# Fused attention and two expert layers on one core: the order of the parts inside a pair of attention heads

## The chip, the cores and the metric

The kernel runs on one core of a Trainium2 chip. The metric is device time in microseconds (us), the median of several executions. The core has five engines that run side by side, each through its own queue in order: TensorE (PE, matmuls; PEld is its weight load), VectorE (DVE), ScalarE (ACT), GpSimd (POOL) and SyncE (SP, which here only issues DMAs). They wait for one another by semaphores.

## What is computed

The reference is an attention over 2 batches of 8 heads, followed by a gated layer and a layer of eight experts. The part that matters here is the attention, which keeps 576 of 1152 queries (each the mean of two neighbours):

```python
q_pool = q.reshape(B, H, S // 2, 2, D).mean(axis=3)      # B, H, S, D = 2, 8, 1152, 64
scores = matmul(q_pool, k.transpose(0, 1, 3, 2)) / sqrt(D)
attn = exp(scores - max(scores, axis=-1))
attn = attn / (sum(attn, axis=-1) + 1e-9)
x = matmul(attn, v)                                       # then reshaped to 1152 x 512
```

After it come `rms`-normalisation, a gated layer (512 to 1536 to 512) and the experts. All inputs and outputs are float32.

## The kernel before

The attention works on eight pairs of heads (`for p in range(NPB)`, line 420), four pairs for each batch. Keys are split into 9 blocks of 128 (`KC`), the 576 queries of a head into 2 groups of 288 (`NG`), so a pair has 18 steps (`NST`). Step i does `st_exp` (lines 197 to 204): for each of the two heads two matmuls into one of three PSUM banks `st`, and an exponential on ACT from that bank into the tile `et`. The score's row maximum is subtracted through an extra column of `Ql`: `s1` (line 182) computes a block of 128 queries against all keys into one single buffer of three banks, and DVE's reduction at line 193 takes the maximum. The next `s1` can only start when that reduction has ended.

Around each `st_exp` other parts are laid. Each step has two places, an even one straight after `st_exp` and an odd one at its end, so there are 36 slots; the tables `S_...` (lines 400 to 416) give the slot of each part:

- `kq_trans` (line 148) transposes keys and queries of the next pair on PE through a single PSUM bank, tag `T`, and ACT evacuates it. `ql_trans` and `ql_trans2` do the same with `Ql`.
- `split` (line 127) splits keys and queries of the pair after the next into a rounded part and a rest: five POOL instructions for each head (lines 108 to 123).
- `esum` (line 207) adds the `et` tiles up; `S_EP` says which of the nine blocks POOL adds (1) and which DVE adds (0). `emerge` (line 219) adds POOL's sum to DVE's, `sums` and `sums2` bring the sums into place.
- `avmm` (line 223) multiplies values by `et` into one bank `av`. It runs in bursts, at the steps with `c % 3 == S_AV`, and takes all `et` tiles up to two steps before (`S_LAG`). In the trace each of its matmuls is two instructions, so a step's two heads are four.
- For the first batch, `x1` (line 273), `xr` (line 293), `x2` and `x2b` turn the result into the next layer's input during pairs 4, 5 and 6 (counted from 0). `x1` and `x2b` use the bank `T` too. `xr` holds a chain of six short instructions: one on DVE, a power on POOL, four on DVE.
- During pair 7, the last one, the next layer's first weights are decoded: `w_dec` (line 380) does for one matrix an absolute value on ACT (step 0), four DVE instructions (steps 1 to 3), and a rounding copy on ACT with a subtraction on POOL (step 4). The work tile `wm` has one buffer there.

After the eight pairs the gated layer starts with matmuls `gv` (line 528); `sums` and `sums2` of the last pair come into its first slots. Its order and the experts' are not part of the change.

Of the kernel before, what the change touches and what calls it, by code (L numbers as in the profile page):

```python
# [9 lines left out]
F32 = mybir.dt.float32  # L10
# [11 lines left out]
def fused_kernel(ctx, tc, q, k, v, w_gate, w_val, w_out, rms_g,  # L22
                 r_gate, r_noise, noise, e_w1, e_w2, out, dbg=None):
    nc = tc.nc
    P = 128
    B, H, S, D = q.shape
    NP = H // 2
# [5 lines left out]
    NG = 288  # L33
# [28 lines left out]
    NPB = B * NP  # L62
# [4 lines left out]
    ab = ax.enter_context(tc.tile_pool(name="ab", bufs=1))  # L67
# [127 lines left out]
    xT, rs, es, ET, AV, accp, smS = {}, {}, {}, {}, {}, {}, {}  # L195

    def st_exp(p, g, c):
        et = ET[p, g, c] = ab.tile([P, 2, NG], F32, name="et", tag="et", bufs=7)
        cs, n0 = slice(c * P, (c + 1) * P), g * NG
        for h in range(2):  # L200
            t = ps[0].tile([P, 512], F32, name="st", tag="st", bufs=3)
            pe.matmul(t[:, 0:NG], KT[p, h][:, cs], QhT[p, h][:, n0:n0 + NG], start=True, stop=False)  # L202
            pe.matmul(t[:, 0:NG], KT2[h][p % NKT[h]][:, cs], QlT[p, h][:, n0:n0 + NG], start=False, stop=True)  # L203
            act.activation(et[:, h, :], t[:, 0:NG], AF.Exp, scale=SCALE)  # L204

    def esum(p, g, c):
# [58 lines left out]
    XS, SS, YY = {}, {}, {}  # L265
# [27 lines left out]
    def xr(b):  # L293
        ss, y = SS[b], YY[b]
        dve.tensor_scalar(y[:, 0], ss, 1.0 / (H * D), 1e-6, op0=ALU.mult, op1=ALU.add)
        pool.tensor_tensor(y[:, 1], y[:, 0], mhalf, op=ALU.pow)
        dve.tensor_tensor(y[:, 2], y[:, 1], y[:, 1], op=ALU.mult)
        dve.tensor_tensor(y[:, 2], y[:, 2], y[:, 0], op=ALU.mult)
        dve.tensor_scalar(y[:, 2], y[:, 2], -0.5, 1.5, op0=ALU.mult, op1=ALU.add)
        dve.tensor_tensor(y[:, 2], y[:, 2], y[:, 1], op=ALU.mult)  # L300
# [96 lines left out]
            act.copy(hi, mf)  # L397
            pool.tensor_tensor(lo, mf, hi.bitcast(F32), op=ALU.subtract)  # L398

    S_S1A = (0, 3, 13, 18, 22)  # L400
    S_S1B = (7, 9, 26, 27, 32)
    S_KA = (1, 3, 6, 9)
    S_KB = (4, 21, 22, 20)
    S_QA = (14, 32)
    S_QB = (24, 33)
    S_SPA = 11
    S_SPB = 24
    S_EM = (2, 21)
    S_SUM = (11, 17)
    S_LD = (4, 34, 34)  # L410
    S_AV = 1
    S_X = (31, 2, 8, 24, 26, 34)
    S_X2 = (4, 8, 20, 24)
    S_EP = (1, 1, 0, 0, 0, 1, 0, 0, 1)
    S_EV = (1, 1, 1, 0, 1, 0, 1, 0)
    S_LAG = 2
    S_W = (0, 0, 13, 26)
    EPL = [[c for c in range(KC) if S_EP[c] == z] for z in range(2)]
    av_q, n_av = [], 0
    for p in range(NPB):  # L420
        F = [[] for _ in range(2 * NST)]

        def at(i, f, *a):
            F[i].append((f, a))

        if p + 1 < NPB:
            at(S_LD[0], load_v, p + 1)
            for i in range(2, QC):
                at(S_S1A[i], s1, p + 1, 0, i - 2)
                at(S_S1B[i], s1, p + 1, 1, i - 2)  # L430
            for i in range(4):
                at(S_KA[i], kq_trans, p + 1, 0, i)
                at(S_KB[i], kq_trans, p + 1, 1, i)
            at(max(S_KA), kt2_copy, p + 1, 0)
            at(max(S_KB), kt2_copy, p + 1, 1)
            at(S_QA[1], ql_trans, p + 1, 0)
            at(S_QB[1], ql_trans, p + 1, 1)
        at(S_S1A[0], s1, p, 0, 3)
        at(S_S1B[0], s1, p, 1, 3)
        at(S_S1A[1], s1, p, 1, 4)  # L440
        at(S_QA[0], ql_trans2, p)
# [12 lines left out]
        if p:
            at(S_EM[0], emerge, p - 1, 1)
            at(S_SUM[0], sums, p - 1)
            at(S_SUM[1], sums2, p - 1)
        at(S_EM[1], emerge, p, 0)
        if p == NP:
            at(S_X[0], x1, 0, 0)  # L460
        if p == NP + 1:
            for i in range(1, QC):
                at(S_X[i], x1, 0, i)
            at(S_X[5], xr, 0)
        if p == NP + 2:
            for t, s_ in enumerate(S_X2):
                at(s_, x2, 0, t)
                at(s_ + 4, x2b, 0, t)
        if p == NPB - 1:
            fr_s.close()  # L470
            wps.append(ctx.enter_context(tc.tile_pool(name="wp", bufs=1, side="right", reuse_waits="tile")))
            for i in range(2):
                at(S_W[0], w_load, 0, i)
                for k_ in range(5):
                    at(S_W[1 + i] + 2 * k_, w_dec, 0, i, k_)
                at(S_W[1 + i] + 6, w_load, 1, i)
            for k_ in range(4):
                at(min(S_W[3] + 2 * k_, 35), w_dec, 1, 0, k_)
        for i in range(NST):
            g, c = divmod(i, KC)  # L480
            st_exp(p, g, c)
            av_q.append((p, g, c))
            for f, a in F[2 * i]:
                f(*a)
            if len(av_q) > 1:
                esum(*av_q[-2])
            if c % 3 == S_AV:
                while n_av < len(av_q) - S_LAG:
                    avmm(*av_q[n_av])
                    n_av += 1  # L490
            for f, a in F[2 * i + 1]:
                f(*a)
# [731 lines left out]
    Y_XR = 9  # L1224
# [243 lines left out]
```

## Time and profile before

| | us |
|---|---|
| median of 3 runs (830.9 to 833.09) | 831.72 |
| the profiled execution | 833.25 |
| span of its instructions | 831.1 |
| PE busy in the span | 788.2 (95%) |
| DVE busy | 578.8 (70%) |
| ACT busy | 421.3 (51%) |
| POOL busy | 304.1 (37%) |

The span is counted from the first to the last instruction, and a trace's times are from its start. Times below come from this one execution. A matmul's row lasts longer than its share of the engine, since the next one starts before it ends; how fast PE goes is read from start to start. "Granted clock" is the share of TensorE's full 2.4 GHz that the core was given in a stretch; it has two levels here, 1.0 and 0.5. A row of a stretch gives from and to, the length, then busy us (and instructions) of PE, PEld, DVE, ACT and POOL, the granted clock, the DMA engines' share and GB/s.

### The profile page before, as it was taken

The page shows a single profiled execution, that of the slowest core. Times are in us where ns is not written, and L with a number is a line of the kernel's source. Part 1 is how long each engine was busy: PE and PEld are TensorE (multiplying, and loading weights), DVE is VectorE, ACT ScalarE, POOL GpSimd, SP SyncE. Part 2 cuts the span into 40 slices and gives each one's busy share as a digit, 9 for nine tenths or more (in the row PEclk, how much of TensorE's full clock was granted, in tenths as well). Part 3 has the DMA queues.
Part 4 walks back from the last instruction along what each step waited for, and adds up shares of the span by engine and source line. Part 5 has one row for each costly group of instructions (what it writes and reads, how often), then busy time and mean ns, then how long its engine had stood idle before and what let it go on. Part 6 is the DMA issues. An engine that isn't in the chain of part 4 may idle for free.

```text
span 831.1 us, 14029 instructions
## 1 busy us (share of the span) xinstructions
PE 788.2 (95%) x5282; PEld 678.8 (82%) x5282; DVE 578.8 (70%) x838; ACT 421.3 (51%) x823; POOL 304.1 (37%) x251
## 2 busy tenths in 40 slices
PE   5999999999898889999999999999999999999992
PEld 4877777777676679999999999889989899998992
DVE  6668667677679676657588737598577869687750
ACT  4655655656566555352233343455465656566530
POOL 8747647648324451222122200102142413424431
PEclk9999999999999899999999999999999999999996
DMA  7345222131131211333123014558989779797311
GB/s 210 85 135 155 51 96 83 47 97 29 41 120 51 101 52 52 100 103 102 52 101 106 1 52 141 182 199 298 368 281 307 268 254 347 229 363 257 106 52 43
DMA packets 72939, 118.83 MB, mean 143 GB/s; under 512 B 7582, under 2 KB 37278, under 8 KB 72864
## 3 DMA queue, kind: packets, MB, share of 16 engines
q1 hardware_dynamic: 67504, 101.55, 37.9%
q0 software_dynamic: 5360, 16.31, 5.6%
q8 instruction: 43, 0.70, 0.3%
q14 instruction: 32, 0.26, 0.1%
HBM read 103.66 MB, written 10.77 MB: 138 GB/s over the span
## 4 chain that ended last, share of the span: by engine, by line
PE 72%; DVE 10%; issue 5%; ACT 4%; POOL 4%; DMA 3%; another core or an unknown queue 1%; POOLq 0%; DVEq 0%; ACTq 0%
PE gv L528 14%; PE py L1100 13%; PE ph L1073 11%; PE po L549 7%; PE av L229 7%; PE st L202 4%; PE s L188 3%; PE st L203 3%; PE tt L135 2%; PE ph L1088 2%; DMA xg<-XD,gidx 2%; DVE Ql L193 1%; PE xt L973 1%; DVE es L217 1%; ACT et L204 1%
## 5 line engine op out<-in xcount | busy, mean ns | idle before, releaser
L528 PE MATMUL gv<-XN,ws 128*128 128x256 f32 (+1 forms) x1152 | 167.4, 298 | 4.1 <-ACT sl L536 3.8
L528 PEld LDWEIGHTS gv<-XN,ws 128*128 128x128 f32 x1152 | 159.1, 190 | 10.1 <-ACT sl L536 4.0
L1006 DVE TENSOR_TENSOR wz<-raw,wz 128x1024 fp32r<-128x1024 f32 x112 | 134.1, 1222 | 14.2 <-ACT wz L106 10.5
L193 DVE TENSOR_REDUCE Ql<-s 128x1 fp32r<-128x1152 f32 x72 | 97.3, 1355 | 58.3 <-PE s L188 44.5
L1100 PE MATMUL py<-wz,hTT 128*128 128x512 f32 x552 | 134.1, 394 | 0.0
L204 ACT ACTIVATE et<-st 128x288 f32<-128x288 f32 x288 | 103.3, 413 | 53.9 <-PE st L203 49.4
L106 ACT CAST wz<-raw 128x1024 fp32r<-128x1024 f32 x112 | 113.5, 1046 | 8.0 <-PE py L1100 8.0
L1100 PEld LDWEIGHTS py<-wz,hTT 128*128 128x128 f32 x552 | 100.7, 188 | 20.2 <-DVE hTT L978 0.6
L398 POOL TENSOR_TENSOR ws<-wm,ws 128x1024 fp32r<-128x1024 f32 x18 | 43.3, 2405 | 150.2 <-ACT ws L397 96.3
L202 PE MATMUL st<-QH,KT 128*128 128x288 f32 x288 | 91.7, 333 | 5.5 <-ACT et L204 4.0
L1073 PEld LDWEIGHTS ph<-xgT,wz 128*128 128x128 f32 x768 | 92.5, 189 | 0.6
L1073 PE MATMUL ph<-xgT,wz 128*128 128x256 f32 x768 | 92.7, 281 | 0.0
L549 PE MATMUL po<-ws,hT 128*128 128x512 f32 x324 | 83.0, 395 | 0.1
L203 PE MATMUL st<-QlT,KT 128*128 128x288 f32 x288 | 82.3, 300 | 0.0
L229 PE MATMUL av<-et,v 128*64 128x288 f32 x576 | 81.9, 420 | 0.0
L202 PEld LDWEIGHTS st<-QH,KT 128*128 128x128 f32 x288 | 55.4, 193 | 20.8 <-ACT et L204 11.5
L217 POOL TENSOR_TENSOR accp<-accp,et 128x576 f32<-128x576 f32 x32 | 48.4, 1513 | 57.3 <-ACT et L204 36.7
L1134 POOL DMA_INDIRECT out_dram<-yo,sidx x23 | 33.1, 1441 | 95.4 <-DVE yo L1133 46.5
L549 PEld LDWEIGHTS po<-ws,hT 128*128 128x128 f32 x324 | 58.4, 188 | 10.7 <-ACT hT L538 0.5
L538 ACT CAST hT<-sl 128x256 fp32r<-128x256 f32 (+1 forms) x48 | 20.8, 433 | 89.4 <-DVE sl L537 89.4
L229 PEld LDWEIGHTS av<-et,v 128*64 128x64 f32 x576 | 37.5, 138 | 26.0 <-issue 5.9
L203 PEld LDWEIGHTS st<-QlT,KT 128*128 128x128 f32 x288 | 55.9, 194 | 0.0
(250 smaller groups left out, 1137.3 us busy)
## 6 DMA issues: line engine op xcount, KB each, us to landing
raw<-in_moe_w_dram SPq DMA_DIRECT2D x112, 512.0 KB
wraw<-in_moe_w_gate_dram SPq DMA_DIRECT2D x6, 1024.0 KB
wraw<-in_moe_w_val_dram SPq DMA_DIRECT2D x6, 1024.0 KB
wraw<-in_moe_w_out_dram SPq DMA_DIRECT2D x6, 1024.0 KB
kraw<-in_k_dram SPq DMA_DIRECT2D x16, 288.0 KB
v<-in_v_dram SPq DMA_DIRECT2D x8, 576.0 KB
KT<-KT SPq DMA_DIRECT2D x16, 288.0 KB
Qraw<-in_q_dram SPq DMA_DIRECT2D x16, 256.0 KB
```

The lines of the kernel that those rows point to most:

```text
L106: act.copy(o, i)
L193: dve.tensor_reduce(Ql[p % 3][h][:, c, D:D + 1], t[:, :, 0:384], axis=AX.XY, op=ALU.max, negate=True)
L202: pe.matmul(t[:, 0:NG], KT[p, h][:, cs], QhT[p, h][:, n0:n0 + NG], start=True, stop=False)
L203: pe.matmul(t[:, 0:NG], KT2[h][p % NKT[h]][:, cs], QlT[p, h][:, n0:n0 + NG], start=False, stop=True)
L204: act.activation(et[:, h, :], t[:, 0:NG], AF.Exp, scale=SCALE)
L217: eng.tensor_tensor(acc, acc, e, op=ALU.add)
L229: pe.matmul(av[h * D:(h + 1) * D, 0:NG], V[p][:, h, c, :], ET[p, g, c][:, h, :], start=(c == 0), stop=(c == KC - 1))
L528: pe.matmul(t[:, 0:n], w[a][:, d, j * P:(j + 1) * P], XN[hf][b_][:, d, cs], start=(k_ == 0), stop=(k_ == 11))
L549: pe.matmul(pt, HT[f, hf][a][:, j, c0:c0 + P], w[b_][:, j, :], start=(k_ == 0), stop=(k_ == 5))
L1006: eng.tensor_tensor(lo, RAW[u % 2][i], hi.bitcast(F32), op=ALU.subtract)
L1073: pe.matmul(o, w[a][:, d, j * P:j * P + P], XT[u][c][:, d], start=z + d == 0, stop=z == 2 and d == 3)
L1100: pe.matmul(PL[u, "y", k], x[c][:, f0 + d, k * P:k * P + P], w[a][:, d], start=i == 4 and z + d == 0, stop=i == 7 and z == 2 and d == 1)
```

## The change

Nothing is computed otherwise, and the same instructions run on PE and ACT. Six things change:

1. The tables of slots have new numbers for nearly all parts.
2. `S_AV` is now a list of steps, (1, 5, 10, 13): four bursts of values' matmuls in a pair instead of six. They cover 6, 4, 5 and 3 steps; in the first pair there are three. `et` gets nine buffers instead of seven.
3. `S_EP` gives block 0 to DVE, so POOL adds two instructions fewer in a pair, and DVE two more.
4. `xr` is cut in two: its first two instructions stay in pair 5, the four last ones (`xr2`) come in pair 6 (`S_XR = 41` is slot 5 of pair 6).
5. The last pair has its own slots (`S_LAST`), with five bursts.
6. The weights' steps in the last pair have slots of their own (`S_W`); ACT's rounding copies are further from DVE's last step before them.

The core of the diff:

```diff
-        et = ET[p, g, c] = ab.tile([P, 2, NG], F32, name="et", tag="et", bufs=7)
+        et = ET[p, g, c] = ab.tile([P, 2, NG], F32, name="et", tag="et", bufs=9)
...
         pool.tensor_tensor(y[:, 1], y[:, 0], mhalf, op=ALU.pow)
+
+    def xr2(b):
+        y = YY[b]
         dve.tensor_tensor(y[:, 2], y[:, 1], y[:, 1], op=ALU.mult)
...
-    S_SPA = 11
-    S_SPB = 24
+    S_SPA = 24
+    S_SPB = 20
...
-    S_AV = 1
-    S_X = (31, 2, 8, 24, 26, 34)
+    S_AV = (1, 5, 10, 13)
+    S_X = (26, 10, 26, 27, 30, 33)
+    S_XR = 41
...
-    S_EP = (1, 1, 0, 0, 0, 1, 0, 0, 1)
+    S_EP = (0, 1, 0, 0, 0, 1, 0, 0, 1)
...
-    S_W = (0, 0, 13, 26)
+    S_W = ((1, 3, 4, 5, 8), (12, 18, 19, 20, 27), (30, 31, 32, 34))
+
+    S_LAST = dict(s1a=(0, 9), s1b=(12,), qa=(15,), em=(16, 28), sum=(20, 35), av=(1, 5, 7, 13, 16))
...
-            if c % 3 == S_AV:
+            if i in sl["av"]:
```

What stands in a row on the engines shows it best. **PE, the first burst of a pair in the middle** (`st` are the scores, `tt` a transpose, `av` the values' matmuls). Before:

```order
L202 MATMUL st<-QH_101,KT 128x288
L203 MATMUL st<-QlT,KT_00_97 128x288
L202 MATMUL st<-QH_101,KT 128x288
L203 MATMUL st<-QlT,KT_01_99 128x288
L229 MATMUL av<-et,v 64x288 x6
L135 MATMUL tt<-identr,khl 128x128 x4
```

The same place in the changed program, with the burst behind a transpose of queries:

```order
L202 MATMUL st<-QH_102,KT 128x288
L203 MATMUL st<-QlT,KT_10_98 128x288
L202 MATMUL st<-QH_102,KT 128x288
L203 MATMUL st<-QlT,KT_11_100 128x288
L135 MATMUL tt<-identr,qh_1297 128x128 x4
L229 MATMUL av<-et,v 64x288 x12
```

The burst at the start of a pair has twelve matmuls instead of six; the transpose of keys that came behind it has gone elsewhere.

**DVE, from the end of pair 5 into pair 6** (`yy` is the chain of `xr`, `Ql` the reduction after an `s1`). Before:

```order
L217 TENSOR_TENSOR es<-es,et 128x2x288
L295 TENSOR_SCALAR yy_2100<-ss_2099 128x5
L297 TENSOR_TENSOR yy_2100<-yy_2100 128x5
L298 TENSOR_TENSOR yy_2100<-yy_2100 128x5
L299 TENSOR_SCALAR yy_2100<-yy_2100 128x5
L300 TENSOR_TENSOR yy_2100<-yy_2100 128x5
L217 TENSOR_TENSOR es<-es,et 128x2x288
L193 TENSOR_REDUCE Ql_91<-s_2587 128x1
```

In the changed program the row begins with the chain's first instruction, and the reduction stands inside the chain:

```order
L295 TENSOR_SCALAR yy_2071<-ss_2070 128x5
L217 TENSOR_TENSOR es<-es,et 128x2x288
L193 TENSOR_REDUCE Ql_91<-s_2585 128x1
L300 TENSOR_TENSOR yy_2071<-yy_2071 128x5
L301 TENSOR_TENSOR yy_2071<-yy_2071 128x5
L302 TENSOR_SCALAR yy_2071<-yy_2071 128x5
L303 TENSOR_TENSOR yy_2071<-yy_2071 128x5
```

The four instructions that need POOL's power have moved behind pair 6's first reduction.

**ACT, the second weight matrix in the last pair** (`wm` is the absolute value, `ws` the rounding copy, `et` the exponentials). Before:

```order
L387 ACTIVATE wm<-wraw 128x1024
L204 ACTIVATE et<-st 128x288 x2
L181 CAST QlT<-tt 128x2x192
L204 ACTIVATE et<-st 128x288 x6
L234 COPY xT<-av 128x288
L397 CAST ws<-wm 128x1024
```

In the changed program the same two instructions, `wm` first and `ws` last, stand further apart:

```order
L390 ACTIVATE wm<-wraw 128x1024
L204 ACTIVATE et<-st 128x288 x2
L181 CAST QlT<-tt 128x2x192
L204 ACTIVATE et<-st 128x288 x6
L248 COPY smS<-sm 128x320
L204 ACTIVATE et<-st 128x288 x6
L234 COPY xT<-av 128x288
L400 CAST ws<-wm 128x1024
```

Between the absolute value and the rounding copy there are now fourteen exponentials, where there were eight.

## Rows read from the trace of the kernel before

**Rows 1.** The page: busy time of each engine.

```profile
PE 788.2 (95%) x5282; PEld 678.8 (82%) x5282; DVE 578.8 (70%) x838; ACT 421.3 (51%) x823; POOL 304.1 (37%) x251
```

**Rows 2.** Stretches: pairs 2 and 4 to 7; busy us by engine, then clock.

```profile
80.96:112.38 31.42, 31.15 (x224) 23.59 (x223) 22.55 (x24) 18.87 (x53) 19.12 (x16) 1.00 0.27 77
...
143.81:176.72 32.91, 31.64 (x229) 23.88 (x228) 24.45 (x27) 19.43 (x55) 20.38 (x17) 1.00 0.25 73
176.72:210.45 33.73, 33.20 (x241) 25.15 (x239) 24.59 (x28) 21.52 (x61) 25.26 (x20) 1.00 0.14 36
210.45:248.75 38.30, 34.96 (x241) 26.69 (x239) 27.11 (x34) 23.57 (x61) 9.62 (x7) 0.96 0.29 87
248.75:282.64 33.89, 28.79 (x175) 19.41 (x175) 29.53 (x28) 19.90 (x47) 14.64 (x8) 0.90 0.19 63
```

**Rows 3.** Timeline, PE, around bursts: start, us, instruction.

```profile
83.07 0.29 PE L203 MATMUL st<-QlT,KT 128*128 128x288 f32 x1
83.29 1.68 PE L229 MATMUL av<-et,v 128*64 128x288 f32 x12
84.90 0.53 PE L135 MATMUL tt<-identr,khl 128*128 128x128 f32 x4
...
96.47 0.40 PE L202 MATMUL st<-QH,KT 128*128 128x288 f32 x1
96.71 0.30 PE L203 MATMUL st<-QlT,KT 128*128 128x288 f32 x1
96.84 0.29 PE L202 MATMUL st<-QH,KT 128*128 128x288 f32 x1
...
121.14 1.19 PE L229 MATMUL av<-et,v 128*64 128x288 f32 x8
```

**Rows 4.** Timeline, PE, a wait between two steps of pair 2.

```profile
103.40 0.29 PE L203 MATMUL st<-QlT,KT 128*128 128x288 f32 x1
103.81 0.40 PE L202 MATMUL st<-QH,KT 128*128 128x288 f32 x1
```

**Rows 5.** Timeline, ACT, six exponentials in a row; behind the time, the idle before them.

```profile
138.93 2.11 ACT L204 ACTIVATE et<-st 128x288 f32<-128x288 f32 x6 [2.70 <-PE st L203]
```

**Rows 6.** Timeline, PE, pair 4, behind the first `x1`.

```profile
173.85 0.45 PE L135 MATMUL tt<-identr,Ql 128*128 128x128 f32 x3 [1.00 <-DVE xs L286]
```

**Rows 7.** Timeline, DVE and PE at the start of pair 6.

```profile
212.37 1.38 DVE L297 TENSOR_TENSOR yy<-yy 128x5 f32<-128x5 f32 x1 [1.31 <-POOL yy L296]
...
217.50 0.62 PE L190 MATMUL s<-KT,QH 128*128 128x384 f32 x1 [2.59 <-DVE Ql L193]
```

**Rows 8.** A stretch just after it (columns as in group 2).

```profile
218.00:220.00 2.00, 2.00 (x8) 2.00 (x7) 0.35 (x2) 0.00 (x0) 0.00 (x0) 0.50 0.00 0
```

**Rows 9.** Timeline, all engines, the last pair.

```profile
256.20 0.79 PE L188 MATMUL s<-KT,QH 128*128 128x384 f32 x3 [1.21 <-DVE Ql L193]
...
259.69 2.38 POOL L398 TENSOR_TENSOR ws<-wm,ws 128x1024 fp32r<-128x1024 f32 x1 [6.09 <-ACT ws L397]
259.72 2.97 DVE L215 TENSOR_TENSOR es<-et 128x576 f32<-128x576 f32 x1
...
271.30 1.05 ACT L397 CAST ws<-wm 128x1024 fp32r<-128x1024 f32 x1 [2.93 <-DVE wm L394]
...
272.71 0.61 PE L202 MATMUL st<-QH,KT 128*128 128x288 f32 x1 [3.80 <-ACT et L204]
```

**Rows 10.** Stretch from the last pair's start to its `sums` (columns as in group 2).

```profile
248.75:287.09 38.34, 33.24 (x209) 22.90 (x207) 31.20 (x30) 22.44 (x51) 16.30 (x9) 0.91 0.25 83
```

**Rows 11.** Groups by line: additions of `et` tiles; busy, mean ns, idle before.

```profile
L217 POOL TENSOR_TENSOR accp<-accp,et 128x576 f32<-128x576 f32 x32 | 48.4, 1513 | 57.3 <-ACT et L204 36.7 <-DVE es L217 14.0 <-DVE rs L261 4.8
...
L217 DVE TENSOR_TENSOR es<-es,et 128x576 f32<-128x576 f32 x48 | 46.7, 974 | 2.3
```

**Rows 12.** Timeline, POOL: first and last of one `split`'s five instructions.

```profile
123.11 1.02 POOL L108 TENSOR_SCALAR khl<-kraw 128x576 fp32r<-128x576 f32 x1 [5.90 <-PE tt L135]
...
127.13 1.11 POOL L123 TENSOR_TENSOR Ql<-qs,qh 128x256 fp32r<-128x256 f32 x1
```

More of the change, by code (lines that the diff above doesn't have):

```diff
@@ L398, in w_dec @@
             pool.tensor_tensor(lo, mf, hi.bitcast(F32), op=ALU.subtract)
[L400 to L405, printed above, removed]
[L406 to L415 removed]
+    S_S1A = (1, 6, 16, 13, 20)
+    S_S1B = (10, 5, 21, 26, 28)
+    S_KA = (0, 5, 2, 7)
+    S_KB = (8, 18, 12, 20)
+    S_QA = (14, 29)
+    S_QB = (15, 33)
+    S_SPA = 24
+    S_SPB = 20
+    S_EM = (12, 33)
+    S_SUM = (17, 22)
+    S_LD = (4, 34, 34)
+    S_AV = (1, 5, 10, 13)
+    S_X = (26, 10, 26, 27, 30, 33)
+    S_XR = 41
+    S_X2 = (6, 22, 27, 31)
+    S_EP = (0, 1, 0, 0, 0, 1, 0, 0, 1)
     S_LAG = 2
[L417 removed]
+    S_W = ((1, 3, 4, 5, 8), (12, 18, 19, 20, 27), (30, 31, 32, 34))
+    S_LAST = dict(s1a=(0, 9), s1b=(12,), qa=(15,), em=(16, 28), sum=(20, 35), av=(1, 5, 7, 13, 16))
     EPL = [[c for c in range(KC) if S_EP[c] == z] for z in range(2)]
@@ L437, in fused_kernel @@
             at(S_QB[1], ql_trans, p + 1, 1)
[L438 to L441, printed above, removed]
+        sl = S_LAST if p == NPB - 1 else dict(s1a=S_S1A, s1b=S_S1B, qa=S_QA, em=S_EM, sum=S_SUM, av=S_AV)
+        at(sl["s1a"][0], s1, p, 0, 3)
+        at(sl["s1b"][0], s1, p, 1, 3)
+        at(sl["s1a"][1], s1, p, 1, 4)
+        at(sl["qa"][0], ql_trans2, p)
         if p + 2 < NPB:
@@ L454, in fused_kernel @@
         if p:
[L455 to L458, printed above, removed]
+            at(sl["em"][0], emerge, p - 1, 1)
+            at(sl["sum"][0], sums, p - 1)
+            at(sl["sum"][1], sums2, p - 1)
+        at(sl["em"][1], emerge, p, 0)
         if p == NP:
@@ L464, in fused_kernel @@
             at(S_X[5], xr, 0)
+        if p == NP + 1 + S_XR // 36:
+            at(S_XR % 36, xr2, 0)
         if p == NP + 2:
@@ L471, in fused_kernel @@
             wps.append(ctx.enter_context(tc.tile_pool(name="wp", bufs=1, side="right", reuse_waits="tile")))
[L472 to L478, printed above, removed]
+            at(0, w_load, 0, 0)
+            at(0, w_load, 0, 1)
+            for i, a in enumerate(((0, 0), (0, 1), (1, 0))):
+                for k_, s_ in enumerate(S_W[i]):
+                    at(s_, w_dec, *a, k_)
+                if i < 2:
+                    at(S_W[i][3], w_load, 1, i)
         for i in range(NST):
@@ L1251, in fused_kernel @@
     at(Y_XR, xr, 1)
+    at(Y_XR, xr2, 1)
     for i, a in enumerate([(1, 4), (0, 4), (1, 0), (1, 1), (1, 2), (1, 3)]):
```

## The prediction

> **What bounds the kernel now.** I read the page first: PE is busy for 95% of the span [rows 1], so only what PE does or waits for between its matmuls can shorten the attention. Then the stretches pair by pair [rows 2]. A pair in the middle takes 31.42 us; pair 4 takes 32.91, pair 5 33.73, pair 6 38.30, and the last one 33.89 although it prepares no further pair and has a fourth fewer matmul instructions (175 against 224). The clock column says the same: 1.00 in pairs 2, 4 and 5, 0.96 in pair 6, 0.90 in pair 7. So the steady pairs are bounded by PE's own order of work, and pairs 6 and 7 by long waits with a slow clock behind them. Third, PE's timeline tells what a burst of values' matmuls costs beside its work and which waits are left [rows 3, 4, 6]; last, the timelines of pairs 6 and 7 say whom PE waits for [rows 7, 9].
>
> **Bursts.** A burst of twelve instructions takes 84.90 - 83.29 = 1.61 us from its start to the next part's [rows 3]. The piece with eight of them lasts 1.19 against 1.68, so four (one step's two heads) take 0.49 and twelve 1.47: 0.14 is the burst's own. Entering costs 0.09 (0.22 from the last score matmul at 83.07, where 0.13 is the usual distance, 96.71 to 96.84), leaving 0.11 (0.24 from 96.47 to 96.71). A burst costs 0.34 us beside its work. Pairs 0 to 6 have 5 + 6 x 6 = 41 bursts before and 3 + 6 x 4 = 27 now: 14 x 0.34 = 4.8. Pair 0 also hands three more steps on, which end up in pair 7, where I count them again: 3 x 0.49 = 1.5. **Gain 6.2.** That nothing is merged is excluded: the changed order shows bursts of twelve, eight, ten and six.
>
> **Longer stretches without a burst.** In a burst ACT and DVE catch up; outside one, a step of scores alone takes PE 4 x 0.13 = 0.53 us, but its two exponentials take ACT 2 x 2.11 / 6 = 0.70 [rows 5]. There are three `st` banks, so PE waits: in pair 2 0.28 us at 103.40 (0.41 between two starts less 0.13) [rows 4], one of three such waits in the pair, 0.19 to 0.28 each and 0.74 in all. I laid the changed slots out step by step with these durations. Between the bursts of steps 13 and 1 stand six steps, and I find waits of 0.3 and 0.5; `s1` comes twice within two or three steps (steps 3 and 5, 6 and 8) and waits some 0.1 each for the reduction to free its only buffer, and a transpose 0.2 for bank `T`: 1.2, so 0.45 more than today. Bounds: all waits vanish (0.74 gained), or each of 14 steps without a burst costs its 0.17 in full (14 x 0.17 = 2.4, 1.7 more than today). I take 0.45, by the waits of 0.19 to 0.28 that are already there. Six pairs: **loss 2.7** (gain 4.4 to loss 10).
>
> **Additions moved from POOL to DVE.** Two per pair. DVE has 31.42 - 22.55 = 8.9 us idle in a pair; the work of the two is 2 x 0.97 = 1.9 [rows 2, 11]. They are followed by reductions, for which `s1` waits; that is in the step-by-step count above. POOL loses 2 x 1.51. Cost nothing in pairs 0 to 6, hidden by DVE's idle time; without that cover 1.9 a pair. The same addition is 0.5 us shorter on DVE than on POOL. The Trainium skill (Perfetto Trace Analysis, section Optimizing Scalar/DVE Operations) speaks against such a move: the two engines share an SBUF port, so shifting work between them might not help. By that rule DVE would not lose the 1.0 us of blocked time that is taken off in the last pair below; that pair would gain 3.8 instead of 4.8, and the median would come to 820.5.
>
> **`x1` in pairs 4 and 5.** In pair 4 `x1` stands one slot ahead of `ql_trans`, both in bank `T`, and PE waits 1.00 us for DVE to empty it [rows 6]. Now a burst (1.61), a step of scores and an `s1` lie between, more than DVE's reduction and multiplication: **gain 1.0** (0 to 1.2). In pair 5 two `x1` have only one step or one burst behind them, and DVE stands in its reductions: between 0 and two waits like that of pair 4, I take 0.6: **loss 0.6** (0 to 2).
>
> **`xr` cut in two, pair 6.** DVE waited 1.31 us for POOL's power inside the chain, which ran long itself (1.38 for a 128 x 5 tile), and the reduction behind it came so late that PE idled 2.59 us for `Ql` [rows 7]. Behind that the clock was 0.50, its lower level of 1.2 GHz [rows 8]; the pair's column loses 0.04 of 38.30 us, 1.5 [rows 2]. What is queued behind the chain now is the reduction of slot 6, not that of slot 1: before it PE has the twelve-matmul burst (3.1 us by the prices above) and two steps. POOL has done its splits and products some 2 us before by my count. **Gain 2.6 + 1.5 = 4.1** (0 if POOL is later). `x2b` at slots 31 and 35 again shares bank `T` with `ql_trans` at 33 and adds evacuations to the burst-free stretch: **loss 0.6** (0 to 2).
>
> **The last pair.** Here two waits stand: 1.21 us for a reduction behind weights' work on DVE, and 3.80 for an exponential that stood behind ACT's rounding copy, which itself waited 2.93 for DVE [rows 9]. The clock loses (1 - 0.91) x 38.34 = 3.4 up to the `sums` of this pair [rows 10]. Without all three PE would be there after 38.3 - 5.0 - 3.4 = 29.9; one burst less (-0.3), three steps more (+1.5), and within the burst of step 13, which crosses from the first group of queries to the second, a wait for ACT to empty `av` (I take 0.6, by the 0.70 that two exponentials take there [rows 5]) make 31.7. But `sums` also needs DVE to be through with the pair's additions and three matrices' steps. DVE is busy for 31.20 of the 38.34 [rows 10]; it gets 1.9 more and loses about 1 that it spent blocked behind POOL: an addition that began with POOL's 2.38 took 2.97 [rows 9] where 0.97 is the mean [rows 11]. With some 1.4 until the first reduction DVE ends at 31.2 + 1.9 - 1.0 + 1.4 = 33.5. So DVE is what comes late next, and PE reaches `sums` after 33.5, not 31.7: **gain 38.3 - 33.5 = 4.8**. Bounds: 31.7 gives 6.6; with DVE idle for 3.6 (half of today's 7.1) and no less blocked it is 36.7 and gives 1.6.
>
> **Sum.** 6.2 - 2.7 + 1.0 - 0.6 + 4.1 - 0.6 + 4.8 = 12.2 us off the profiled execution's own 833.25 (its span of 831.1 and 2.15 around it, which stays): 821.05. That execution lies 1.53 above the median of the runs, 831.72, so the median should come to **819.5**. The gated layer and the experts keep their order; the slots that follow `sums` hang on it and shift with it.
>
> **Rivals.**
> - *The waits stay in the last pair.* ACT's rounding copy of the second matrix again waits for DVE, or the absolute value of the third waits for POOL's subtraction (one `wm` buffer). For: DVE is the fuller engine there, and POOL and DVE block each other [rows 9]. Against: the copy stands six slots further from DVE's step. The last pair then gains 0.8 instead of 4.8: 823.5. The Trainium skill (SBUF — State Buffer, section Who interferes with whom) states that a DVE instruction with two SBUF inputs and a reading GpSimd one exclude each other for their whole length; it would make this case likelier, and the 2.97 us row agrees.
> - *POOL's power is late in pair 6.* The wait of 2.6 and its slow clock stay: 819.5 + 4.1 = 823.6. For: POOL is fullest in pair 5 (25.26 us) [rows 2]; against: three additions there become two in each group.
> - *Better than counted.* No added waits in the steady pairs, pairs 5 and 6, and the last pair bounded by PE: 819.5 - 2.7 - 1.2 - 1.8 = 813.8.
> - *Slower.* The two `split` now stand at steps 10 and 12 instead of 5 and 12, one behind the other on POOL, with an addition behind. One takes 5.13 us (123.11 to 128.24) [rows 12], two 10.3, with the addition (1.51) 11.8; from step 10, at some 17.5 us of 31, they end at 29.3. The next pair transposes them in its slots 0 and 2, from 31 on. If POOL is slowed by DVE until both take over 15 us, PE waits at the start of each of six pairs; it decides from 2.5 us a pair on (12.2 gained and 2.5 for a slower verdict, over six). At 3 us: 819.5 + 18 = 837.5. Against: POOL's share of a pair is 19.12 of 31.42 and falls.
>
> **How the numbers follow.** Forecast with its own spread (816 to 822.5) 0.52; waits stay in the last pair 0.18; power late 0.08; better 0.13; slower 0.05; gains and losses within 0.3% of no change 0.04. A measurement of this kernel can tell about 0.3%, 2.5 us, from no change. Faster 0.91, same 0.04, slower 0.05. The range for 8 in 10 takes in the better case down to 812 and both cases of waits that stay, together with a steady loss near the middle of its bounds, up to 827.
>
> **What would show it.** Pairs 1 to 3 at about 31.1 us each, with bursts of 24, 16, 20 and 12 instructions; no wait above 1 us for `Ql` at the start of pair 6 and a clock of 1.00 there; pair 4 near 31.9; in the last pair no wait above 2 us and a clock of 0.97 or more, and `sums` behind DVE's last merge. I am wrong if steady pairs take over 31.4 (the longer stretches cost more than the bursts), if PE waits for `khl` at a pair's start, or if the clock falls again in pairs 6 or 7.

## The result, and the profile after

| | before | changed |
|---|---|---|
| median of 4 runs each, us | 832.04 (830.9 to 833.09) | 821.94 (817.62 to 823.64) |
| the profiled execution, us | 833.25 | 823.6 |
| its span, us | 831.1 | 821.8 |
| pair 0, us | 30.26 | 27.98 |
| pairs 1, 2, 3 | 31.38, 31.43, 31.43 | 30.87, 30.86, 30.85 |
| pairs 4, 5, 6 | 32.91, 33.73, 38.30 | 31.31, 34.34, 34.17 |
| pair 7 up to its `sums` | 38.34 | 34.09 |
| `sums` reached at | 287.09 | 273.80 |
| from there to the last `gv` matmul of the gated layer | 242.35 | 243.97 |
| from there to the end (experts) | 301.70 | 304.07 |

The time is 0.9866 of that before, interval [0.984, 0.9892]; a second set of runs gave 0.987 [0.9833, 0.9906]. The forecast was 819.5, its range 812 to 827. The lengths of pairs are read from the trace, from the first score matmul of one to that of the next. They shrink by 13.3 us in all, more than the 12.2 that the sum had; 4 us of this are given back behind the attention. A second profile of the same changed kernel reaches `sums` at 274.90, 12.2 us earlier than before. The difference between the two profiles is nearly all in pair 0, which takes 29.18 us there: a stretch of slow clock at its start lasts 6.8 us in that execution and 3.4 in the one of the table and in the kernel before (clock over the pair 0.89, against 0.94 in the other two).

The page of the changed kernel, busy time of each engine (to lay beside [rows 1]):

```profile
PE 782.5 (95%) x5282; PEld 678.4 (83%) x5282; DVE 584.0 (71%) x854; ACT 416.7 (51%) x823; POOL 281.4 (34%) x235
```

DVE has 16 instructions more and 5 us more to do, POOL 16 fewer and 23 us less. PE has as many instructions as before and is busy for 5.7 us less; slow stretches of its clock count as busy.

Stretches of the changed kernel, pairs 2 and 4 to 7, the last up to its `sums` (columns as in [rows 2], which they answer, and [rows 10]):

```profile
78.18:109.04 30.86, 30.71 (x224) 23.59 (x223) 22.80 (x27) 18.29 (x52) 15.99 (x15) 1.00 0.26 71
139.90:171.20 31.30, 31.14 (x228) 24.07 (x227) 23.81 (x29) 18.92 (x54) 16.44 (x16) 1.00 0.29 80
171.20:205.54 34.34, 33.22 (x240) 25.32 (x239) 28.37 (x33) 20.63 (x60) 21.27 (x18) 1.00 0.17 47
205.54:239.71 34.17, 32.77 (x240) 25.30 (x239) 26.88 (x35) 22.96 (x61) 10.35 (x7) 1.00 0.32 97
239.71:273.80 34.09, 31.52 (x222) 22.26 (x221) 31.86 (x34) 21.71 (x50) 13.78 (x7) 1.00 0.21 66
```

The granted clock is 1.00 in all five; in pairs 6 and 7 it was 0.96 and 0.91. In a steady pair PE is busy for all but 0.15 us.

The four bursts of pair 2, in PE's timeline of the changed kernel, each with what follows it:

```profile
80.90 3.13 PE L229 MATMUL av<-et,v 128*64 128x288 f32 x24
83.96 0.40 PE L202 MATMUL st<-QH,KT 128*128 128x288 f32 x1
...
88.88 2.16 PE L229 MATMUL av<-et,v 128*64 128x288 f32 x16
90.97 0.40 PE L202 MATMUL st<-QH,KT 128*128 128x288 f32 x1
...
97.85 2.65 PE L229 MATMUL av<-et,v 128*64 128x288 f32 x20
100.43 0.79 PE L188 MATMUL s<-KT,QH 128*128 128x384 f32 x3
...
103.83 1.68 PE L229 MATMUL av<-et,v 128*64 128x288 f32 x12
105.44 0.40 PE L202 MATMUL st<-QH,KT 128*128 128x288 f32 x1
```

From start to next start they take 3.06, 2.09, 2.58 and 1.61 us for 24, 16, 20 and 12 instructions. Four instructions cost (3.06 - 1.61) / 3 = 0.48, and 1.61 - 3 x 0.48 = 0.16 belongs to the burst itself, as [rows 3] gave it (0.49 and 0.14).

The start of pair 6 in DVE's timeline of the changed kernel (answers [rows 7]):

```profile
205.57 2.64 DVE L295 TENSOR_SCALAR yy<-ss 128x5 f32<-128x5 f32 x1
208.12 0.74 DVE L217 TENSOR_TENSOR es<-es,et 128x576 f32<-128x576 f32 x1
208.79 1.34 DVE L193 TENSOR_REDUCE Ql<-s 128x1 fp32r<-128x1152 f32 x1
210.06 1.28 DVE L300 TENSOR_TENSOR yy<-yy 128x5 f32<-128x5 f32 x1
```

No wait stands in brackets: DVE doesn't wait for POOL's power inside the chain, and the reduction comes first. The longest waits of PE that are left in pairs 6 and 7, and those at the gated layer's start, in PE's timeline:

```profile
238.28 0.45 PE L135 MATMUL tt<-identr,Ql 128*128 128x128 f32 x3 [0.86 <-DVE XN L320]
...
260.68 1.68 PE L229 MATMUL av<-et,v 128*64 128x288 f32 x12 [0.50 <-ACT xT L234]
...
273.80 0.74 PE L245 MATMUL sm<-es,ones 128*32 128x320 f32 x8 [2.01 <-DVE es L221]
...
290.07 2.70 PE L536 MATMUL gv<-XN,ws 128*128 128x256 f32 x12 [3.73 <-ACT sl L544]
293.38 4.81 PE L536 MATMUL gv<-XN,ws 128*128 128x256 f32 x24 [0.61 <-DVE sl L545]
```

The waits of 2.59 in pair 6 [rows 7] and of 1.21 and 3.80 in the last pair [rows 9] are gone. Ahead of `sums` PE waits 2.01 us for DVE's last merge, as the forecast said (its sign was 2 at most). The wait of 0.50 at 260.68 is the one for ACT to empty `av`, for which the forecast had 0.6. The wait of 3.73 at 290 has a counterpart in the kernel before, and it stands at the same distance, 16.3 us, behind `sums` (PE's timeline of the kernel before):

```profile
303.40 2.93 PE L528 MATMUL gv<-XN,ws 128*128 128x256 f32 x12 [3.77 <-ACT sl L536]
```

### The profile page after: what moved, and what is told of

It reads as the page before. It is cut to its first block, busy times and chain, and to the rows that moved or that the text cites. A ratio compares the mean times of both kernels' runs of the same rounds, so it can differ in the third digit from the quotient of the medians.

```text
span 821.8 us, 14014 instructions
## 1 busy us (share of the span) xinstructions
PE 782.5 (95%) x5282; PEld 678.4 (83%) x5282; DVE 584.0 (71%) x854; ACT 416.7 (51%) x823; POOL 281.4 (34%) x235
## 4 chain that ended last, share of the span: by engine, by line
PE 78%; DVE 7%; DMA 5%; ACT 4%; issue 3%; POOL 1%; POOLq 0%; ACTq 0%; DVEq 0%
PE gv L536 14%; PE py L1108 12%; PE ph L1081 11%; PE av L229 9%; PE po L557 8%; PE st L202 5%; PE s L188 5%; PE st L203 4%; DMA xg<-XD,gidx 4%; PE tt L135 2%; ACT et L204 1%; PE ph L1096 1%; PE xt L981 1%; DVE Ql L193 1%; DVE wz L1014 1%
## 5 line engine op out<-in xcount | busy, mean ns | idle before, releaser
L229 PE MATMUL av<-et,v 128*64 128x288 f32 x576 | 77.4, 412 | 0.5 <-ACT xT L234 0.5
L217 DVE TENSOR_TENSOR es<-es,et 128x576 f32<-128x576 f32 x64 | 59.7, 933 | 1.5
```

The lines of the kernel that those rows point to most:

```text
L217: eng.tensor_tensor(acc, acc, e, op=ALU.add)
L229: pe.matmul(av[h * D:(h + 1) * D, 0:NG], V[p][:, h, c, :], ET[p, g, c][:, h, :], start=(c == 0), stop=(c == KC - 1))
```

## Experiments

### Bursts and slots apart

Six bursts on the changed kernel's slots:

```diff
-    S_AV = (1, 5, 10, 13)
+    S_AV = (1, 4, 7, 10, 13, 16)
```

> The changed kernel with its new slots, but six bursts of values' matmuls in pairs 0 to 6 again (the last pair keeps its five). Theory (a burst costs 0.34 us beside its work): pairs 1 to 3 go from 30.86 back to about 31.5 us, pair 0 gets two bursts and three steps more (+2.1), the whole is 5 to 6 us slower than the changed kernel (821.9): 827 to 828. Rival (the gain of pairs 1 to 3 comes from the new slots, the merging brings nothing): pairs 1 to 3 stay at 30.9, only pair 0 pays its three steps (1.5, given back in pair 7): 822 to 823.

And the other way round, the kernel before with four bursts and nine buffers, all slots as they were:

```diff
-...name="et", tag="et", bufs=7)
+...name="et", tag="et", bufs=9)
...
-    S_AV = 1
+    S_AV = (1, 5, 10, 13)
...
-            if c % 3 == S_AV:
+            if i in S_AV:
```

> The kernel before with its old slots, but bursts at steps 1, 5, 10 and 13 and nine buffers of exponentials. Theory (0.34 us for a burst): pairs 1 to 3 at 30.8 instead of 31.42, pair 0 about 2.1 shorter, the waits of pairs 6 and 7 untouched: 5 to 6 us faster than before, 826 to 827. Rival (merging needs the new slots, since longer stretches without a burst make PE wait for ACT): pairs 1 to 3 at 31.3 to 32, the whole 830 to 833.

Measured: 829.14 us with six bursts (0.9928 [0.9895, 0.9961] of the kernel before) and 851.22 with four bursts on the old slots (1.0204 [1.0157, 1.025]). Pair 2 of the six bursts, then, from the second kernel, of the four (stretches, columns as above):

```profile
82.19:113.83 31.64, 30.97 (x225) 23.53 (x224) 24.46 (x26) 18.61 (x53) 16.39 (x15) 1.00 0.27 74
```

```profile
84.76:119.18 34.42, 31.21 (x225) 23.70 (x223) 23.16 (x24) 18.63 (x53) 19.11 (x16) 1.00 0.24 70
```

So pair 2 gives a table of two by two, all with a clock of 1.00:

| pair 2, us | old slots | new slots |
|---|---|---|
| six bursts | 31.43 | 31.64 |
| four bursts | 34.42 | 30.86 |

Neither half is a gain alone. On the old slots fewer bursts cost 3.0 us a pair, which neither the theory nor the rival had; the new slots with six bursts cost 0.2. Together they bring 0.57. On the new slots two bursts less are worth 31.64 - 30.86 = 0.78, where 2 x 0.34 = 0.68 had been expected. But this is not the price of two bursts alone: with six bursts PE waits once in each of pairs 1 to 3 for the reduction that frees the buffer of `s1`, where the changed kernel is late for an `s1` by 0.2 at most (PE's timeline of six bursts, pair 2):

```profile
94.43 0.79 PE L188 MATMUL s<-KT,QH 128*128 128x384 f32 x3 [0.63 <-DVE Ql L193]
```

What PE waited for in pairs 1 to 4 of four bursts on the old slots (us in all, how often, the longest):

```profile
PE tt L135 <- DVE rs L261: 5.7, 4, 1.4
PE tt L135 <- ACT QlT L141: 3.3, 4, 1.4
PE tt L135 <- DVE Ql L193: 2.5, 3, 0.8
```

These are 11.5 us, where the four pairs are 13.4 longer. In the first two lines a transpose shares bank `T` with the one ahead of it and waits until that has been evacuated; in the third it waits for the reduction that writes a column of `Ql`. Between the two transposes of the second line a burst of 1.6 us stands in the kernel before (at 109.76 of its pair 2). Between those of the first line none stood there. What is seen there is that DVE is late with the evacuation (`rs`), with two additions ahead of it that ran beside POOL's: 3.32 us for two, where one took 0.74 above (timeline of the same kernel, pair 2):

```profile
100.47 3.32 POOL L217 TENSOR_TENSOR accp<-accp,et 128x576 f32<-128x576 f32 x2
101.09 3.32 DVE L217 TENSOR_TENSOR es<-es,et 128x576 f32<-128x576 f32 x2
```

The next kernel asked whether the loss hangs on these places: the four bursts on the old slots with two transposes moved.

```diff
-    S_KB = (4, 21, 22, 20)
-    S_QA = (14, 32)
+    S_KB = (4, 21, 22, 23)
+    S_QA = (14, 29)
```

> The kernel before with four bursts and nine buffers (which took 851.2, pairs 1 and 2 at 34.4 and a wait of some 1.5 us in each for bank T), and two slots of the preparation moved: kq_trans of the second head's last tile from slot 20 to 23 (behind the burst of step 10), ql_trans of the first head from 32 to 29. Theory (a removed burst was the cover under which VectorE and ScalarE emptied bank T for the next transposes, so the loss sits at these few slots): the two waits of 1.5 and 0.7 to 0.8 us go, pairs 1 and 2 come to 32.0 to 33.0, the time to 836 to 842. Rival (the loss is the longer stretches themselves, spread over all steps): the waits only move to other transposes, pairs 1 and 2 stay above 34, the time at 848 to 853.

Measured: 851.28 us (1.0196 [1.0164, 1.0229]), pairs 1 and 2 at 33.66 and 33.67. The theory falls in this form; the time is the rival's, and the waits moved to other transposes as the rival had it. The wait for `rs` is gone, but others took its place (PE's waits of the moved kernel, the same 140 us):

```profile
PE tt L135 <- DVE Ql L193: 6.9, 5, 1.5
PE tt L135 <- ACT QH L141: 2.7, 4, 0.7
```

The transposes of `Ql` now reach PE ahead of DVE's reduction. That two places carry the loss is refuted: of the 3.0 us in pair 2 their move brought back 0.75. That a removed burst was the cover is read from the order of the rows in one of these places, and no run shows it by itself. Which of the new slots are needed stays open.

### The cut of `xr` alone

The kernel before with `xr` in two, the second half in slot 5 of pair 6, and the first `x2` moved behind it.

```diff
+    def xr2(b):
+        y = YY[b]
...
-    S_X2 = (4, 8, 20, 24)
+    S_X2 = (6, 8, 20, 24)
...
+            at(5, xr2, 0)
```

> The kernel before with the chain of xr cut alone: its four last instructions in slot 5 of pair 6, x2(0) and x2b(0) two slots later so that they stand behind them. Theory: the wait of 2.6 us for Ql at the start of pair 6 and the slow clock behind it go, pair 6 falls from 38.3 to about 34.2, the whole by 4.1: 828. Rival (POOL is late with the power wherever the chain stands): the wait comes back at the reduction of the next s1, pair 6 stays at 37 to 38, 831 to 832.

Measured: 830.98 us (0.9958 [0.9937, 0.9978]). Pair 6 is 35.28 long instead of 38.30, at a clock of 1.00:

```profile
210.45:245.73 35.28, 33.13 (x241) 25.17 (x239) 26.21 (x34) 23.39 (x61) 10.19 (x7) 1.00 0.31 94
```

The gain is 3.0, not 4.1. Both the wait of 2.59 and the slow clock went, as expected; a new wait stands in their place, the longest of PE's waits in that pair:

```profile
PE sm L245 <- DVE XN L320: 1.4, 1, 1.4
```

It comes from this experiment's own edit: the first `x2b` went with its `x2` from slot 8 to slot 10, straight ahead of `sums` at slot 11, and both use bank `T` (the `x2b` starts at 221.49, DVE evacuates it at 222.75, `sums` starts at 223.50). Without that wait the cut would bring 3.0 + 1.4 = 4.4, by estimate. In the changed kernel `sums` is at slot 17, and that wait is not there; pair 6 gains 4.1.

### The last pair alone

The kernel before with `S_LAST`, `S_W` and nine buffers; the old division of additions stays.

```diff
-    S_W = (0, 0, 13, 26)
+    S_W = ((1, 3, 4, 5, 8), (12, 18, 19, 20, 27), (30, 31, 32, 34))
+    S_LAST = dict(s1a=(0, 9), s1b=(12,), qa=(15,), em=(16, 28), sum=(20, 35), av=(1, 5, 7, 13, 16))
...
-            if c % 3 == S_AV:
+            if i in sl["av"]:
```

> The kernel before with the last pair's own slots and the weights' slots alone (nine buffers, the additions divided as before). Theory: the waits of 1.21 and 3.80 us and their slow clock go; from the last pair's start to its sums 34 to 35 us instead of 38.34, with a wait of 1 to 3 us for DVE's last merge in front of sums; the whole 3.5 to 4.5 us faster: 828. Rival (the last pair needs POOL's relief by the new division of the additions): 36 to 38 us to sums, 830 to 832.

Measured: 831.12 us (0.9975 [0.9949, 1.0001]). The median alone shows no gain, since the interval reaches 1.0001; the stretches do. The pair reaches `sums` after 34.05, as in the changed kernel, and PE waits as long (1.97) in front of it for DVE's last merge:

```profile
249.23:283.28 34.05, 30.73 (x210) 21.45 (x209) 32.01 (x31) 21.98 (x51) 16.84 (x9) 1.00 0.20 64
283.28:527.22 243.94, 239.52 (x1588) 222.48 (x1589) 159.95 (x297) 94.89 (x180) 52.15 (x40) 0.99 0.26 87
```

The 4.3 us are all in `S_LAST` and `S_W`. But 1.6 of them are lost at once: from `sums` to the last `gv` it is 243.94, where it was 242.35. The new tables of the pairs before are not needed for this loss.

### The changed kernel once more, and with the old division of additions

> The changed kernel once more, for a second profile beside the next three. Theory (the 2.4 us lost behind the gated layer are waits for gathered rows, which differ from execution to execution and are not the change's): the attention ends as before (sums at 273.8 us), the rest of the span differs by 1 to 3 us. Rival (the change itself moves those waits): the stretch behind the gated layer is again 304 us, where the kernel before has 301.7.

Measured: 823.73 us (0.987 [0.9833, 0.9906]); pair 2 at 30.84, pair 7 at 34.12, from `sums` on 244.01 and 304.92. The experts again take 304.9, which is the rival's sign; what the other kernels show of it stands further down. `sums` comes at 274.90 and not at 273.8, for the clock in pair 0.

```diff
-    S_EP = (0, 1, 0, 0, 0, 1, 0, 0, 1)
+    S_EP = (1, 1, 0, 0, 0, 1, 0, 0, 1)
```

> The changed kernel with the old division of the additions of exponentials: steps 0, 1, 5 and 8 of a group on GpSimd, not 1, 5 and 8, in all pairs; all else as changed. Theory (the prediction's: VectorE's idle time hides the two additions a pair): pairs 1 to 3 stay within 0.1 us of 30.86, the last pair at 34.1, the time within 0.3% of the changed kernel's 821.9. Rival A (the moved additions are part of the gain): GpSimd is late with its additions and splits, the steady pairs go above 31.0 and the time to 824 or more. Rival B (the moved additions cost something, VectorE being the engine that sets the last pair): the last pair becomes shorter than 33.8 and the time falls by over 0.5 us.

Measured: 824.99 us (0.9894 [0.9864, 0.9923]), which can't be told from the changed kernel. Two stretches, pair 5 and pair 7 up to its `sums`:

```profile
171.81:206.97 35.16, 33.23 (x240) 25.32 (x239) 27.94 (x30) 20.73 (x60) 25.28 (x21) 1.00 0.19 54
...
241.43:275.39 33.96, 31.52 (x223) 22.26 (x221) 32.63 (x32) 21.82 (x50) 16.97 (x9) 1.00 0.20 64
```

Pairs 1 to 3 are 30.86 to 30.93 long: the two additions cost nothing there and bring nothing, as the theory said. The median lies in the range of rival A, but its sign, steady pairs above 31.0, did not come. In pair 5 they bring 0.8: with POOL's share at 25.28, PE waits 1.0 us for DVE in front of a transpose, where the changed kernel has 0.2. In the last pair nothing is gained (33.96 against 34.09), although DVE is busy for 0.8 less with two instructions more.

### The third matrix out of the last pair

Three steps of DVE on the third weight matrix go from the last pair to the first slots of the gated layer.

```diff
-    S_W = (..., (30, 31, 32, 34))
+    S_W = (..., (30,))
...
+    for k_ in range(3):
+        at(k_, w_dec, 1, 0, 1 + k_)
```

> The changed kernel with DVE's steps for the third weight matrix taken out of the last pair and placed in slots 0 to 2 of the gated layer, behind the last merge. Theory (DVE's queue sets the last pair's end): the wait of 2.0 us in front of sums goes, from the last pair's start to sums 32.1 instead of 34.1; 2 us faster than the changed kernel if the slow clock behind it stays as it is. Rival (POOL's last addition or PE's own order sets it): sums still waits 1 to 2 us, no change.

Measured: 820.62 us (0.9857 [0.983, 0.9884]). The pair reaches `sums` 2.1 us earlier, and all of it is gone at the last `gv`, which starts at 517.77 in the changed kernel and at 517.78 here:

```profile
239.84:271.85 32.01, 31.45 (x222) 22.21 (x221) 29.38 (x32) 21.71 (x50) 13.98 (x7) 1.00 0.21 67
271.85:517.78 245.93, 239.61 (x1590) 222.38 (x1590) 162.11 (x299) 94.45 (x179) 52.06 (x40) 0.99 0.26 86
```

The waits of PE behind it (timeline):

```profile
275.01 0.55 PE L255 MATMUL xt<-ident,smS 128*128 128x128 f32 x3 [1.51 <-ACT smS L248]
289.92 2.42 PE L536 MATMUL gv<-XN,ws 128*128 128x256 f32 x12 [3.81 <-ACT sl L544]
293.21 6.41 PE L536 MATMUL gv<-XN,ws 128*128 128x256 f32 x36 [0.88 <-DVE sl L545]
```

The long wait ends at 289.92, in the changed kernel at 290.07. The gain is gone as early as the first of these rows: the same transposes of `sums2` start at 275.01 here and at 275.30 in the changed kernel, where no wait stands in front of them. DVE has the same weight work to do either way; now it stands behind the last merge (until 273.87), and the copy `smS` for which PE waits stands on ACT behind a copy that needs DVE. What releases the wait at 290 is the next question.

### The start of the gated layer

At 290 ACT's `sl` stands behind the rounding copy of matrix (1, 1), which waits 2.55 us for DVE's step 3. The first attempt put that matrix's last three steps and the second half of the norm's chain (`xr2` of batch 1) further back; a second one joined it with the third matrix's move.

```diff
-    at(Y_XR, xr2, 1)
+    at(13, xr2, 1)
...
+    for k_, s_ in enumerate((5, 6, 12, 13, 17)):
+        at(s_, w_dec, 1, 1, k_)
```

> The changed kernel with another order at the start of the gated layer, 16 us behind sums: DVE's last two steps and ACT's copy for matrix (1, 1) at slots 12, 13 and 17 instead of 7, 8 and 9, and the second part of xr for batch 1 at slot 13 instead of 9. Theory (PE's wait of 3.7 us there is ACT's copy standing in front of the activation, and the slow clock behind it costs 3.4 us in this profile, 1.7 in that of before): the wait falls to under 1 us, the clock stays at 1.00, 5 to 7 us faster. Rival (DVE is simply full there): the wait comes back within the next 5 us with at least 2.5 us, gain under 2 us.

> The edits of the two runs before this one together. Theory: the gains add up, 7 to 9 us faster than the changed kernel, 813 to 815 us. Rival (with the third matrix's steps in the first slots DVE is late at the start of the gated layer): only one of the gains, 816 to 820.

Measured: 823.11 (0.9878 [0.9855, 0.9901]) and 823.96 us (0.989 [0.9865, 0.9915]). In the first the rival's sign came, a wait of over 2.5 us within 5 us of the old one. Its reason, that DVE is full, is not what the row names: PE now waits for ACT's copy of the matrix itself, later and longer (PE's timeline of the first of the two):

```profile
294.67 2.07 PE L536 MATMUL gv<-XN,ws 128*128 128x256 f32 x8 [5.33 <-ACT ws L400]
```

For both edits together neither the theory nor the rival held: of the gains none is left.

The next two leave the matrix where it was and move only `xr2` of batch 1, by three slots; the second also has the third matrix's move.

```diff
-    at(Y_XR, xr2, 1)
+    at(Y_XR + 3, xr2, 1)
```

> The changed kernel with the second half of the norm's chain of the second batch (xr2) three slots later in the gated layer, so that it stands behind VectorE's next product of the gated layer. Theory (the chain held VectorE from 288.7 to 293.0, and with it the product for which TensorE waited a second time, 0.6 us, and this is why the slow clock of that stretch lasts 6.8 us and not 3.4): the second wait goes, the stretch of slow clock at 290 lasts 3.4 us, the last matmul of the gated layer starts 2 us earlier against the sums (242.0 instead of 243.97), the time falls by about 2 us to 820. Rival (the first wait of 3.7 us alone slows the clock): the stretch stays 6.8 us long and the time within 0.7 us of the changed kernel's.

> Both: the third weight matrix's three steps on VectorE moved from the last pair into the first slots of the gated layer (alone it brought the last pair to 32.0 and the time to 820.6), and xr2 of the second batch three slots later. Theory: the sums stay at 271.9, the wait of 3.8 us at 290 stays (it hangs on VectorE's queue), the wait behind it goes; the last matmul of the gated layer 2 us earlier than in either, the time 818 to 820. Rival: VectorE's queue as a whole decides, the last matmul of the gated layer stays at 517.8, the time at 820 to 822.

Measured: 819.57 (0.9827 [0.9791, 0.9862]) and 819.41 us (0.9826 [0.9797, 0.9856]). In both the second wait is gone. Of the changed kernel, DVE and POOL at that place:

```profile
290.05 2.34 DVE L300 TENSOR_TENSOR yy<-yy 128x5 f32<-128x5 f32 x1 [1.30 <-POOL yy L296]
...
292.91 0.42 DVE L545 TENSOR_TENSOR sl<-gv,sl 128x256 f32<-128x256 f32 x1
...
289.98 2.39 POOL L401 TENSOR_TENSOR ws<-wm,ws 128x1024 fp32r<-128x1024 f32 x1
```

and of the last kernel, DVE:

```profile
289.86 0.42 DVE L545 TENSOR_TENSOR sl<-gv,sl 128x256 f32<-128x256 f32 x1 [1.31 <-ACT sl L544]
...
290.76 1.70 DVE L547 TENSOR_TENSOR hT<-sl,hT 128x256 fp32r<-128x256 f32 x1 [0.47 <-ACT hT L546]
...
292.38 0.15 DVE L300 TENSOR_TENSOR yy<-yy 128x5 f32<-128x5 f32 x1
```

The product `sl` for which PE waits comes at 289.86 instead of 292.91, and the same 128 x 5 instruction takes 0.15 us away from POOL's subtraction and 2.34 beside it. The time beside POOL did not vanish: now the product `hT` meets the subtraction (289.79 to 292.18) and takes 1.70 instead of 0.43, but PE doesn't wait for it there. Stretches of 20 us over this place, the third matrix moved alone and then with `xr2` behind:

```profile
283.00:303.00 20.00, 15.32 (x104) 14.42 (x103) 12.58 (x22) 8.72 (x20) 6.17 (x4) 0.83 0.14 54
```

```profile
283.00:303.00 20.00, 16.19 (x123) 15.58 (x122) 12.53 (x25) 10.36 (x24) 6.16 (x4) 0.91 0.15 54
```

The clock is 0.91 instead of 0.83, and 19 more matmuls fit. From `sums` to the last `gv` it is 243.70 instead of 245.93: 2.2 us, as the theory had it. With `xr2` alone the clock rises there too (0.91 from 285 to 305), but a stretch of slow clock at 275, right behind the wait for `sums`, took 1.7 back, so that only 0.4 is left (243.52). In the changed kernel and in four others the same wait of 1.9 to 2.0 has no slow clock behind it (with six bursts one of 2.4 has); why it has one here is open. These two are the fastest kernels that were run. Their ratios lie 0.4% under the changed kernel's, and the intervals overlap.

## Why the prediction was right, and where its steps were not

**Bursts: right in sign, the price too high.** Pair 0 gained 2.28, by the sum 2 x 0.34 + 1.47 = 2.15; in the second profile of the changed kernel, with the longer slow stretch, it gained 1.08, so only the profile with the same clock as before agrees. The 0.78 of the six bursts is near 0.68 by luck, since it holds the wait of 0.63. Counted by late starts of PE (the distance of two starts less the usual one), pair 2 with six bursts has waits of 0.19, 0.80, 0.13 and 0.17, together 1.29, and the changed kernel 0.83; the two bursts together are then worth some 0.78 - 0.46 = 0.3 and not 0.68, an estimate.

**Longer stretches without a burst: too much.** The sum took 0.45 a pair away and left 0.68 - 0.45 = 0.23; pairs 1 to 3 gained 0.51 to 0.58. In pair 2 of the changed kernel PE's starts are late at five places, by 0.28, 0.06, 0.19, 0.13 and 0.17: 0.83 in all. The prediction had 0.74 in the kernel before, but left one place out, 0.14 at 107.97; counted alike they are 0.19, 0.27, 0.28 and 0.14, 0.88. So the waits did not grow, and the loss of 2.7 for six pairs has no counterpart in this pair. The gain of 0.57 is then that of two bursts fewer, some 0.26 each by estimate, with 0.34 in the sum. Both terms were too large, with opposite signs. What I had not seen is how much the old slots needed their bursts: that the same merging costs 3 us a pair without the new tables was in none of the cases.

**`x1`.** Pair 4 gained 1.6, by the sum 1.23; pair 5 lost 0.61, by the sum 0.37. Right in sign and place. The sum gave the moved additions nothing; they are why the wait in pair 5 is 0.2 and not 1.0.

**`xr` and pair 6: right in mechanism, 4.1 for 3.7 (4.1 - 0.6 + 0.23).** No wait for `Ql` above 1 us, a clock of 1.00. Alone the cut brings 3.0, since that kernel moved an `x2b` in front of `sums` and waits 1.4 for it. The 0.86 that PE waits at 238 is for the `x2b` of slot 31, for which I had 0.6.

**The last pair: right in number by luck, wrong in its reason.** It took 34.09, the forecast 33.5, and `sums` waits for DVE's last merge. I had got there by DVE's work as a whole: busy time plus some idle time at the start. But with two additions less for DVE the pair is as long. What sets the end is where the third matrix's steps stand: ACT's absolute value of slot 30 ends at 265.7, DVE waits 0.63 for it, and then its four instructions, two additions and the last merge follow each other (DVE's timeline of the changed kernel):

```profile
265.70 1.20 DVE L392 TENSOR_SCALAR wm<-wm 128x1024 f32<-128x1024 f32 x1 [0.63 <-ACT wm L390]
...
270.56 1.21 DVE L397 SCALAR_TENSOR_TENSOR wm<-wraw,wm 128x1024 int32<-128x1024 int32 x1
...
272.90 0.76 DVE L221 TENSOR_TENSOR es<-es,accp 128x576 f32<-128x576 f32 x1 [0.25 <-issue]
```

With those steps gone the pair takes 32.0, near the 31.7 that I had for PE alone. The second matrix's copy waits no longer; it stands seven slots behind DVE's step instead of two, five further and not six. DVE's time beside POOL was not saved either: an addition at 262.13 took 2.94 beside POOL's subtraction, as the 2.97 of [rows 9].

**"The slots that follow `sums` hang on it and shift with it": the step that failed.** Attention ends 13.3 us earlier, the last `gv` starts 11.7 earlier. The 1.6 between them is a slow clock that lasts longer behind the wait at 290, although that wait is as long as before (3.73 and 3.77). The 20 us around it, in the changed kernel:

```profile
283.00:303.00 20.00, 15.66 (x106) 14.75 (x105) 12.74 (x22) 8.65 (x20) 6.35 (x4) 0.83 0.15 54
```

and in the kernel before:

```profile
296.00:316.00 20.00, 15.87 (x119) 14.97 (x119) 13.43 (x23) 9.45 (x22) 6.66 (x5) 0.91 0.16 54
```

In the changed kernel and seven other profiles with the new last pair the slow stretch lasts 6.8 us instead of 3.4; at half speed the difference costs 1.7. It is back at 3.4 in the two kernels with `xr2` moved by three slots, where the second wait is gone; so the runs tie the length to that wait. That is not the whole rule: the kernel before has a second wait too (0.37) and a short stretch, while the six bursts with the same 0.37 and, with the old last pair, the four bursts with two transposes moved (0.36) have a long one. What else decides is open. And the 2.1 us that the third matrix's move gained at `sums` were worth nothing at the last `gv`, since DVE's work came back in front of what the gated layer waits for.

**The experts, 2.4.** They took 304.07 instead of 301.70. PE's waits there, of the changed kernel:

```profile
PE xt L981 <- DMA xg<-XD,gidx: 3.0, 4, 0.9
```

In the kernel before this wait has 0.5. In the twelve other profiles the same part takes 298.9 to 304.9, with 0.3 to 1.9 us of this wait; the changed kernel's own second profile has 304.9 with 1.2, so this wait alone does not make the difference. None of the kernels changes the order there, and the six later variants of the changed kernel have 298.9 to 303.2. So I put it down to the execution and not to the change. That is argued and not shown: both profiles of the changed kernel itself lie at 304 to 305, and what makes it is open.

Together: 13.3 gained at `sums` - 1.6 - 2.4 = 9.3 in the profiled executions; the medians differ by 10.1. That the median lies only 2.4 us above the forecast is in part luck: 1.1 more than the sum was gained in the attention, 4.0 that it did not have were lost behind it. Of the rivals none occurred as a whole: no wait for `khl` at a pair's start, no wait for POOL's power, and the two waits in the last pair are gone. Of the better case one part came, no added waits in the steady pairs.

The rule from the Trainium skill (Perfetto Trace Analysis, Optimizing Scalar/DVE Operations) that moving work between GpSimd and VectorE may not help comes out half: the last pair was no shorter for it (34.09 and 33.96), while DVE was busy for 31.86 us with the additions and 32.63 without, and pair 5 gained 0.8.

## What to carry to other kernels

A slot table and the grouping of a filler belong together: before a burst is removed, look which evacuation it covered, and place anew whatever shares a bank with its neighbours. When a wait in one stage is removed, follow the queue of the engine that releases the next stage, since a gain that this queue does not share is given back at its head. A tiny VectorE instruction that meets a large one on GpSimd can last as long as that (2.34 us here); when the bottleneck waits for what stands behind it, put it further back.

## What was not expected of the hardware

A 128 x 5 multiplication on VectorE took 2.34 us, from 290.05 to 292.39, while GpSimd's subtraction ran from 289.98 to 292.37, and 0.15 where GpSimd was idle. The Trainium skill (SBUF — State Buffer, Who interferes with whom) says that the one that issues first gets the shared port for its whole instruction and the other blocks; this pair of rows agrees to 0.02 us. At 205.57 one of 128 x 5 with a single tensor input took 2.64 us, to 208.21, past the end of one GpSimd instruction (206.79) and to the end of the next (208.18): it did not get its turn between the two. That is not always so: the addition at 262.13 ended at 265.07, after one GpSimd instruction (264.46) and before the end of the next (264.42 to 266.35). What decides is open.
